# Attention and mixer kernel: the last row tile leaves in two halves of the channels

## The chip, the cores and the metric

The kernel runs on one core of one Trainium2 chip. The metric is the device time of one execution in microseconds (us). The profile of an execution reports its span, which is shorter: in the six runs of the changed kernel the time is 1.75 to 2.5 us longer than the span.

TensorE does the matmuls. VectorE and ScalarE read its sums from PSUM, the memory that holds them. SyncE starts most of the transfers. Rows of a profile name the engines PE, PEld (weight loads), DVE (VectorE), ACT (ScalarE), POOL (GpSimd) and SPq or ACTq (the instruction queues of SyncE and ScalarE).

## The reference

Block-sparse attention over 4 batches, 8 heads, 768 positions and 64 dimensions is followed by a low-rank token mixer and a two-layer perceptron over 512 channels.

```python
scores = scale * np.matmul(q, k.transpose(0, 1, 3, 2))     # scale = 1/8
scores = np.where(mask, scores, -1000000000.0)             # block mask
attn = np.exp(scores - np.max(scores, axis=-1, keepdims=True))
attn = attn / (np.sum(attn, axis=-1, keepdims=True) + 1e-09)
x = heads_side_by_side(np.matmul(attn, v))                 # (4, 768, 512)
h = x.transpose(0, 2, 1) @ U @ V                           # rank 32
u = x + h.transpose(0, 2, 1)
out = u + np.maximum(u @ w_ch1, 0.0) @ w_ch2               # 512 -> 2048 -> 512
```

(`heads_side_by_side` stands for a transpose and a reshape.)

## The kernel before

The kernel interleaves the attention of one batch with the perceptron of the batch before, so that TensorE always has work. Behind the last batch there is no more attention, so its perceptron runs alone at the end. The second layer goes by row tiles of 128 positions, T = 6 to a batch (`...` marks lines left out; comments in the cuts are added). Each gathers 16 matmuls of 512 columns in one PSUM buffer, is added to `xf`, and is stored.

```python
        def w2(sc, part):
            if part == 0:
                hold[sc] = psm([P, HD], FP32)          # sums of a row tile; HD = 512
                ...
            for jj in range(4 * part, 4 * part + 4):
                nc.tensor.matmul(
                    hold[sc],
                    bt.tT[jj][:, sc * P : (sc + 1) * P],
                    w2t[:, jj, :],
                    start=(b > 0 and jj == 0), stop=(jj == NJJ - 1),
                )
            if part == 3:
                of = opool.tile([P, HD], FP32, tag="of", name="of")
                nc.vector.tensor_add(out=of, in0=bt.xf[:, sc, :], in1=hold[sc])
                nc.sync.dma_start(
                    out=out[b].rearrange("(p t) d -> p t d", t=T)[:, sc, :], in_=of
                )
```

`opool` has two buffers and `psm` three. TensorE's order is written by hand; the order on the other engines is the scheduler's.

From the seventh pair of heads on (i = 6, counted from 0), Q and K are turned by transposing transfers from SyncE (`front`): in the traces from `qst` and `kst`, where they lie as loaded, into `qres` and `kres`. In the program they come after the loads of V of a later pair:

```python
            if i + 2 < NPAIR:
                last = load_qk(i + 2)
                load_v(i + 2)
                ...
            if i + 1 < NPE:                            # NPE = 6: turned by TensorE
                ...
            elif i + 1 < NPAIR:
                front(i + 1)                           # turned by transfers
```

The softmax here doesn't subtract the row's maximum and nothing guards it: scores larger than these inputs give would overflow.

Of the kernel before, what the change touches and what calls it, by code (L numbers as in the profile page):

```python
# [9 lines left out]
FP32 = mybir.dt.float32  # L10
# [6 lines left out]
P = 128  # L17
# [3 lines left out]
def kernel(  # L21
# [14 lines left out]
    nc = tc.nc  # L36

    B, H, S, D = q.shape
    BLK = 32
    NB = S // BLK  # L40
    T = S // P
    HD = H * D
# [3 lines left out]
    NJJ = CH // P  # L46
# [45 lines left out]
    opool = ctx.enter_context(tc.tile_pool(name="opool", bufs=2))  # L92
# [11 lines left out]
    def psm(shape, dtype):  # L104
        return psmp.tile(shape, dtype, tag="pm", name="pm")
# [20 lines left out]
    w2t = wpool.tile([P, NJJ, HD], FP16)  # L126
# [20 lines left out]
    def load_v(i):  # L147
# [12 lines left out]
        out=sb[0:NB].rearrange("k z r w -> k (z r w)"),  # L160
        in_=sampled_blocks.bitcast(I32).rearrange("z r -> (z r)")[None, :].broadcast_to(
            [NB, NB * 6]
        ),
# [4 lines left out]
    for h in range(2):  # L168
        for src, nm in ((q, "qld"), (k, "kld")):
            if h == 0:  # L170
# [3 lines left out]
                out=lds[nm][:, h], in_=src[0, h].rearrange("(p t) d -> p t d", t=T)  # L174
# [32 lines left out]
    with tc.manual_schedule(  # L207
# [27 lines left out]
        def first_row(n, c, copy):  # L235
# [14 lines left out]
            out=eq[0:NB], in0=sb[0:NB, :, :, 0], scalar1=iota, scalar2=-1.0,  # L250
# [3 lines left out]
            out=a01[0:NB], in_=eq[0:NB], axis=mybir.AxisListType.X, op=ALU.max  # L254
        )
        nc.vector.scalar_tensor_tensor(
            out=bias[0:NB, :, 0:NB], in0=a01[0:NB, None].broadcast_to([NB, 2, NB]),
# [239 lines left out]
    def mlp_steps(b, bt):  # L497
        def w1(jj, c):
            if c == 0:
                bt.tT.append(tpool.tile([P, S], FP16, tag="tT", name="tT"))  # L500
            pt = psm([P, HS], FP32)
            for cc in range(NCC):
                nc.tensor.matmul(  # L503
                    pt,
                    w1t[:, cc, jj * P : (jj + 1) * P],
                    bt.uT[cc][:, c * HS : (c + 1) * HS],
                    start=(cc == 0), stop=(cc == NCC - 1),
                )
            dst = bt.tT[jj][:, c * HS : (c + 1) * HS]
            if c == 0:  # L510
                nc.scalar.activation(out=dst, in_=pt, func=AF.Relu)  # L511
            else:
                nc.vector.tensor_scalar_max(out=dst, in0=pt, scalar1=0.0)  # L513

        hold = {}

        def w2(sc, part):
            if part == 0:
                hold[sc] = psm([P, HD], FP32)
                if b == 0:  # L520
                    nc.tensor.matmul(  # L521
                        hold[sc], Vt[:, sc, :], bt.a16, start=True, stop=False
# [12 lines that stand above are left out]
                    out=out[b].rearrange("(p t) d -> p t d", t=T)[:, sc, :], in_=of  # L535
                )

        steps = [
            (4 * HS, False, lambda jj=jj, c=c: w1(jj, c))
            for jj in range(NJJ)  # L540
            for c in range(2)
        ]
        steps += [
            (
                (5 if b + part == 0 else 4) * HD,
                part < 3,
                lambda sc=sc, part=part: w2(sc, part),
            )
            for sc in range(T)
            for part in range(4)  # L550
        ]
        return steps


# [36 lines left out]
    with tc.manual_schedule(engines={mybir.EngineType.PE}):  # L591
# [7 lines left out]
        for i in range(NPAIR):  # L599
            b, hp = divmod(i, HP)  # L600
            if hp == 0:
                bt = Batch()
# [59 lines left out]
            if hp == HP - 1:  # L662
                coming = mlp_steps(b, bt)
                mixer.append((slot + 9, lambda coming=coming: queue.extend(coming)))
# [37 lines left out]
```

## Time and profile before

| | before |
|---|---|
| time, median of the first 3 runs | 301.82 us (301.35 to 302.26) |
| span of the profiled run | 298.8 us |
| start of the last addition, to the end of the span | 294.36 us, 4.46 us |

The page of the profile gives the busy time of each engine, its share of the span and its count of instructions.

```profile
PE 291.8 (98%) x2758; PEld 181.2 (61%) x2758; DVE 142.4 (48%) x299; ACT 180.1 (60%) x261; POOL 50.1 (17%) x70
```

TensorE bounds the kernel. The chain of work that ended last, with start, duration and group, shows how it ends.

```profile
252.81 20.80 PE pm L503 x128
273.61 20.73 PE pm L525 x96
294.36 0.69 DVE of L533
```

The 96 matmuls of the last second layer (L525) follow one another without a gap, 20.73 us / 96 = 215.9 ns each, or 3.455 us for a row tile of 16. The last addition starts as they end. The timeline of the last 5 us has start, duration, engine, line, operation, operands and, in brackets, the idle time before and what ended it.

```profile
294.36 0.69 DVE L533 TENSOR_TENSOR of<-xf,pm 128x512 f32<-128x512 f32 x1 [2.76 <-PE pm L525]
295.08 0.33 SPq L534 DMA_DIRECT2D out_dram<-of  x1
```

Narrow windows over the same stretch give the busy time of each engine, then the clock, the busy share of the 16 DMA engines and GB/s.

```profile
295.70:295.90 0.20, 0.00 (x0) 0.00 (x0) 0.00 (x0) 0.00 (x0) 0.00 (x0) 1.00 0.00 0
295.90:296.10 0.20, 0.00 (x0) 0.00 (x0) 0.00 (x0) 0.00 (x0) 0.00 (x0) 1.00 0.92 348
296.10:296.30 0.20, 0.00 (x0) 0.00 (x0) 0.00 (x0) 0.00 (x0) 0.00 (x0) 1.00 0.97 369
296.30:296.50 0.20, 0.00 (x0) 0.00 (x0) 0.00 (x0) 0.00 (x0) 0.00 (x0) 1.00 1.00 379
296.50:296.70 0.20, 0.00 (x0) 0.00 (x0) 0.00 (x0) 0.00 (x0) 0.00 (x0) 1.00 0.59 215
296.70:296.90 0.20, 0.00 (x0) 0.00 (x0) 0.00 (x0) 0.00 (x0) 0.00 (x0) 1.00 0.01 0
```

The bytes of the last store move for only 0.7 us, and start 0.8 us after the issue. This tail is serial: addition, issue, transfer, landing, end of the program. Only work in it, and the matmuls ahead of it, can shorten or lengthen the time here.

### The profile page before, as it was taken

To read this page: it belongs to the slowest core of one execution; us is meant where nothing else is said; L and a number is where in the kernel's file an instruction comes from. 1 tells how busy PE (TensorE), PEld (TensorE's weight loads), DVE (VectorE), ACT (ScalarE), POOL (GpSimd) and SP (SyncE) were. 2 spreads that over 40 slices of the span, in tenths; PEclk is the share of its full clock that TensorE was granted. 3 is DMA by queue.
4 is the path that set the end of the run, shared out by engine and by line. 5 is a ranking of instruction groups with operands and counts; after the bars stand their busy time and mean duration, and the time that the engine had idled before them with its cause. 6 is when DMAs were issued, how large, how long until landed. Compare 5 with 4: busy or idle time off the path is not lost.

```text
span 298.8 us, 6750 instructions
## 1 busy us (share of the span) xinstructions
PE 291.8 (98%) x2758; PEld 181.2 (61%) x2758; DVE 142.4 (48%) x299; ACT 180.1 (60%) x261; POOL 50.1 (17%) x70
## 2 busy tenths in 40 slices
PE   8999999999999999999999999999999999999993
PEld 3677776666665655666665556666665555665441
DVE  7766866347452524454552625345462535443121
ACT  4999997577865665777775565777865530332000
POOL 3783197123223030110202010000000000000000
PEclk9999999999999999999999999999999999999999
DMA  6999989989988485634616271613310122000111
GB/s 185 283 353 238 311 253 235 268 206 218 197 245 178 145 163 147 140 107 64 176 29 141 61 162 53 146 23 46 88 29 35 39 61 72 35 0 2 70 70 71
DMA packets 58519, 39.96 MB, mean 134 GB/s; under 512 B 40136, under 2 KB 54872, under 8 KB 58488
## 3 DMA queue, kind: packets, MB, share of 16 engines
q1 hardware_dynamic: 55764, 35.32, 44.2%
q0 software_dynamic: 2688, 4.19, 7.8%
q8 instruction: 21, 0.34, 0.5%
q14 instruction: 10, 0.08, 0.1%
q10 hardware_dynamic: 36, 0.01, 0.0%
HBM read 27.72 MB, written 6.29 MB: 114 GB/s over the span
## 4 chain that ended last, share of the span: by engine, by line
PE 88%; ACT 9%; issue 1%; DVE 0%; ACTq 0%
PE pm L503 28%; PE pm L525 28%; PE psc L380 17%; ACT est L386 9%; PE pv L420 9%; PE pm L442 2%; PE pm L475 1%; PE psc L218 1%; PE pm L362 0%; PE pm L521 0%; PE pm L491 0%; PE psc L200 0%; DVE of L533 0%; PE pm L452 0%; PE pm L200 0%
## 5 line engine op out<-in xcount | busy, mean ns | idle before, releaser
L386 ACT ACTIVATE est<-psc 128x768 f16<-128x768 f32 x192 | 150.3, 810 | 53.0 <-PE psc L380 52.6
L525 PE MATMUL pm<-w2t,tT 128*128 128x512 f16 x384 | 94.1, 379 | 0.0
L503 PEld LDWEIGHTS <-w1t 128*128 128x128 f16 x512 | 47.1, 98 | 27.0 <-issue 0.3
L420 PEld LDWEIGHTS <-est 128*128 128x128 f16 x1152 | 51.9, 97 | 16.5
L513 DVE TENSOR_SCALAR tT<-pm 128x384 f16<-128x384 f32 x64 | 35.6, 557 | 51.3 <-PE pm L503 48.7
L525 PEld LDWEIGHTS <-tT 128*128 128x128 f16 x384 | 34.8, 98 | 32.0
L511 ACT ACTIVATE tT<-pm 128x384 f16<-128x384 f32 x64 | 31.3, 489 | 37.3 <-PE pm L503 18.7
L380 PE MATMUL psc<-qres_102,kres_104 128*128 128x384 f16 x192 | 46.8, 325 | 1.1 <-ACT est L386 0.9
L380 PE MATMUL psc<-qres_103,kres_105 128*128 128x384 f16 x192 | 46.6, 325 | 0.2
L533 DVE TENSOR_TENSOR of<-xf,pm 128x512 f32<-128x512 f32 x24 | 16.4, 684 | 28.7 <-PE pm L525 28.7
L420 PE MATMUL pv<-vt_99,est 128*128 128x65 f16 x576 | 27.9, 193 | 0.0
L420 PE MATMUL pv<-vt_98,est 128*128 128x65 f16 x576 | 27.8, 193 | 0.0
L380 PEld LDWEIGHTS <-kres_105 128*128 128x128 f16 x192 | 18.3, 98 | 13.6 <-issue 0.5
L380 PEld LDWEIGHTS <-kres_104 128*128 128x128 f16 x192 | 18.0, 97 | 14.0 <-issue 2.0
L429 DVE RECIPROCAL rcp<-pv 128x6 f32<-128x6 f32 x32 | 6.2, 193 | 38.6 <-PE pv L420 38.6
L434 DVE TENSOR_TENSOR xh<-pv,rcp 128x384 f16<-128x384 f32 x32 | 17.8, 557 | 1.0
L434 DVE TENSOR_TENSOR xf<-pv,rcp 128x384 f32<-128x384 f32 x32 | 17.5, 548 | 0.0
L481 DVE TENSOR_TENSOR xf<-xf,pm 128x384 f32<-128x384 f32 x24 | 13.1, 547 | 0.0
L144 POOL CAST qst_101<-qld 128x768 f16<-128x768 f32 x5 | 4.1, 828 | 47.3 <-DMA qres_103<-qst_101 47.3
L144 POOL CAST qst_100<-qld 128x768 f16<-128x768 f32 x5 | 4.1, 827 | 39.9 <-DMA qres_102<-qst_100 39.9
L503 PE MATMUL pm<-uT_207,w1t 128*128 128x384 f16 x32 | 10.4, 326 | 0.0
L503 PE MATMUL pm<-uT_989,w1t 128*128 128x384 f16 x32 | 10.4, 326 | 0.0
(125 smaller groups left out, 298.1 us busy)
## 6 DMA issues: line engine op xcount, KB each, us to landing
vld<-in_v_dram SPq DMA_DIRECT2D x16, 384.0 KB, 7.1
out_dram<-of SPq DMA_DIRECT2D x24, 256.0 KB, 2.0
qld<-in_q_dram SPq DMA_DIRECT2D x15, 384.0 KB, 3.5
kld<-in_k_dram SPq DMA_DIRECT2D x15, 384.0 KB, 6.0
w1t<-in_moe_w_ch_dram POOLq DMA_DIRECT2D x4, 512.0 KB, 9.3
w2t<-in_moe_w_ch_dram POOLq DMA_DIRECT2D x4, 512.0 KB, 12.6
qld<-in_q_dram SPq DMA_DIRECT2D x2, 192.0 KB, 3.3
kld<-in_k_dram SPq DMA_DIRECT2D x2, 192.0 KB, 4.3
```

Source lines behind the costliest of these rows:

```text
L144: last = nc.gpsimd.tensor_copy(out=dst, in_=ld)
L380: nc.tensor.matmul(psc[:, c, 0:HS], kT[:, h, g * P : (g + 1) * P], qT[:, h, c * HS : (c + 1) * HS], start=True, stop=True,)
L386: nc.scalar.activation(out=est.rearrange("k (c n) -> k c n", c=2), in_=psc[:, :, 0:HS], func=AF.Exp, scale=0.125,)
L420: nc.tensor.matmul(pav[:, sc, :], est[:, sc * P : (sc + 1) * P], vts[self.b % 2][:, head, g, 0 : D + 1], start=(g == 0 and sc == 0), stop= ...
L429: nc.vector.reciprocal(out=rcp, in_=pav[:, :, D])
L434: self.last = nc.vector.tensor_tensor(out=dst, in0=pav[:, :, 0:D], in1=rcp[:, :, None].broadcast_to([P, T, D]), op=ALU.mult,)
L481: nc.vector.tensor_add(out=xf, in0=xf, in1=pu)
L503: nc.tensor.matmul(pt, w1t[:, cc, jj * P : (jj + 1) * P], bt.uT[cc][:, c * HS : (c + 1) * HS], start=(cc == 0), stop=(cc == NCC - 1),)
L511: nc.scalar.activation(out=dst, in_=pt, func=AF.Relu)
L513: nc.vector.tensor_scalar_max(out=dst, in0=pt, scalar1=0.0)
L525: nc.tensor.matmul(hold[sc], bt.tT[jj][:, sc * P : (sc + 1) * P], w2t[:, jj, :], start=(b > 0 and jj == 0), stop=(jj == NJJ - 1),)
L533: nc.vector.tensor_add(out=of, in0=bt.xf[:, sc, :], in1=hold[sc])
```

## The change

The intent is to overlap most of the last row tile's addition and store with its own matmuls, and to leave only half an addition and half a store behind the last one. The matmuls of the last row tile split into two groups of 256 columns, each with its own sums, addition and store. The second store goes out on ScalarE's queue.

```diff
+        def last_half(c):
+
+            sc = T - 1
+            po = psm([P, HD // 2], FP32)
+            ch = slice(c * HD // 2, (c + 1) * HD // 2)
+            for jj in range(NJJ):
+                nc.tensor.matmul(
+                    po, bt.tT[jj][:, sc * P : (sc + 1) * P], w2t[:, jj, ch],
+                    start=(jj == 0), stop=(jj == NJJ - 1),
+                )
+            of = opool.tile([P, HD], FP32, tag="of", name="of")
+            nc.vector.tensor_add(out=of[:, ch], in0=bt.xf[:, sc, ch], in1=po)
+            (nc.sync, nc.scalar)[c].dma_start(
+                out=out[b].rearrange("(p t) d -> p t d", t=T)[:, sc, ch], in_=of[:, ch]
+            )
+
...
+        if b == B - 1:
+            steps[-4:] = [(8 * HD, False, lambda c=c: last_half(c)) for c in range(2)]
         return steps
```

## The prediction

> **What bounds the kernel now.** TensorE: the page gives PE 98% busy, and the chain of waits is PE for 88% of the span, at clock 1.00. The chain ends with 96 second-layer matmuls in 20.73 us (215.9 ns each). The change touches only the serial tail behind them: in the timeline the last addition starts at 294.36 us and takes 0.69 us; the store's issue starts at 295.08 and takes 0.33 us. In narrow windows the DMA engines move bytes only from 295.9 to 296.6 (0.70 us, about 370 GB/s). The store lands 2.0 us after its issue, near 297.1; the span ends at 298.8. So 4.4 us lie behind the last matmul, 1.7 us of them after the landing.
>
> **What the change does.** The order of instructions differs only in the last row tile: 16 matmuls of 512 columns become two groups of 16 with 256 columns and the weights loaded twice; one addition becomes two of 256 columns; one store becomes two of 128 KB, the last from ScalarE's idle queue.
>
> **On the critical path.**
> - Matmuls: the columns streamed are the same. Matmuls of 512 and 384 columns start 215.9 and 162.3 ns apart, a line with a fixed term of about 2 ns, so 16 more cost about +0.04 us. The extra weight loads (98 ns busy) should hide: in the timeline 65-column matmuls, each with its own load, start 30 ns apart, far below the 109 ns that I estimate for 256 columns.
> - Last addition: 686 ns for 512 columns, 548 ns for 384 in the groups, so about 415 ns for 256. The Trainium skill, "VectorE: DVE Perf Modes", section on the errata, gives (N+151)/0.96 ns, here 424. Gain 0.27 us.
> - Last store: half the bytes at the same rate, 0.35 us of movement; the fixed part of the 2.0 us stays. Gain 0.25 to 0.35 us.
> - Issue from ScalarE instead of SyncE: its only issue in this trace took 0.60 us, for another shape, against 0.33 us. Cost 0 to 0.27 us.
> - First half: its sums end near 292.6, its store lands near 295.2, before the last store's bytes move. It hides. The second half reuses the buffer whose store lands by 293.6, before its addition at 294.4. The separate queue gains nothing: SyncE is idle by then. The skill's "DMA: Bandwidth & Descriptors", section on issuing engines, agrees: another queue saves only issue time.
>
> **Sum.** −0.27 − 0.30 + 0.04 + 0.13 = −0.40 us, between −0.55 and −0.25: 0.13%, less than the scatter of the three runs (301.35 to 302.26). I predict 301.4 us, 300.8 to 302.0 eight times in ten. Chances: faster by over 2% 0.005, within 2% 0.985, slower by over 2% 0.01.
>
> **What would show it.** Right: the last addition starts at 294.40 ± 0.05 and takes 0.41 to 0.43 us; the last store's bytes move for 0.35 to 0.4 us and land 1.65 to 1.75 us after issue; span 298.3 to 298.6; everything before 291 us unchanged. Wrong: 256-column matmuls over 115 ns apart; a second addition that waits for a store instead of PE; ScalarE's issue over 0.6 us; or an end that lengthens because a second queue must be drained.
>
> **What would make it wrong.** Mostly noise between sessions, larger than the effect; then loads that alternate with matmuls (32 × 98 ns = 3.1 us more), or a slower ScalarE issue, which could cancel the gain.

## The result, and the profile after

| | before | changed |
|---|---|---|
| time, median of 6 fast runs | 301.81 us (300.91 to 302.94) | 301.54 us (300.98 to 302.15) |
| ratio of the fast runs | | 0.9991, 95% interval 0.9967 to 1.0016 |
| span of the profiled run | 298.8 us | 299.1 us |
| start of the last addition | 294.36 us | 295.20 us |
| from there to the end of the span | 4.46 us | 3.87 us |

The fast runs of before are the first three and three more. Ratios are the mean time of one kernel's fast runs over that of the other's of the same rounds, so not quite the ratio of the medians. By the times alone the two kernels are the same; a gain of 0.4 us is smaller than what the interval can resolve. The two traces say more. The end of the chain after the change:

```profile
253.60 20.80 PE pm L503 x128
274.40 17.27 PE pm L525 x80
291.67 3.51 PE pm L544 x32
295.20 0.42 DVE of L549
```

The last row tile (L544) takes 3.51 us instead of 3.455; its matmuls start 109 to 110 ns apart in the trace. But the last first layer (L503) starts at 253.60, not 252.81: 0.79 us were lost before the changed code began. The timeline of the tail:

```profile
293.46 0.42 DVE L549 TENSOR_TENSOR of<-xf,pm 128x256 f32<-128x256 f32 x1 [1.06 <-PE pm L544]
293.90 0.33 SPq L550 DMA_DIRECT2D out_dram<-of  x1
295.20 0.42 DVE L549 TENSOR_TENSOR of<-xf,pm 128x256 f32<-128x256 f32 x1 [1.32 <-PE pm L544]
295.65 0.38 ACTq L550 DMA_DIRECT2D out_dram<-of  x1
```

Both additions wait for PE (the brackets), so neither waits for a store. The first half's addition and issue are over before the second half's sums are. Windows over the last store:

```profile
296.40:296.60 0.20, 0.00 (x0) 0.00 (x0) 0.00 (x0) 0.00 (x0) 0.00 (x0) 1.00 0.22 77
296.60:296.80 0.20, 0.00 (x0) 0.00 (x0) 0.00 (x0) 0.00 (x0) 0.00 (x0) 1.00 0.97 333
296.80:297.00 0.20, 0.00 (x0) 0.00 (x0) 0.00 (x0) 0.00 (x0) 0.00 (x0) 1.00 0.73 241
297.00:297.20 0.20, 0.00 (x0) 0.00 (x0) 0.00 (x0) 0.00 (x0) 0.00 (x0) 1.00 0.02 5
```

The busy shares times 0.2 us add up to 0.39 us of movement, against 0.70 before. So the tail became 0.59 us shorter, as meant, and something earlier took it back in this execution. The waits of TensorE after the first 10 us name it. Columns: engine and line, what it waited for, total us, times, longest. First the kernel before, then the changed one.

```profile
PE psc L380 <- ACT est L386: 0.4, 2, 0.2
```

```profile
PE psc L380 <- DMA kres_104<-kst_106: 0.7, 1, 0.7
PE psc L380 <- ACT est L386: 0.4, 2, 0.2
```

The 0.7 us is one wait near 75 us for the transposed load of K. It lies 216 us ahead of the changed code. TensorE's timeline in the changed kernel:

```profile
75.93 0.50 PE L380 MATMUL psc<-qres_102,kres_104 128*128 128x384 f16 x2 [0.68 <-DMA kres_104<-kst_106]
```

More can be read from the two traces. Every engine has the same instructions in the same order in both, up to the last row tile. So each matmul of one can be set against the same matmul of the other: the changed kernel runs 0.05 us early at 74 us, 0.80 us late at 78 us, and 0.80 us late still at 270 us. The whole loss arose at that one wait.

### The profile page after: what moved, and what is told of

Read it like the earlier page. It is cut to its first block, busy times and chain, and to the rows that moved or that the text cites. A ratio compares the mean times of both kernels' runs of the same rounds, so it can differ in the third digit from the quotient of the medians.

```text
span 299.1 us, 6786 instructions
## 1 busy us (share of the span) xinstructions
PE 292.0 (98%) x2774; PEld 182.8 (61%) x2774; DVE 142.5 (48%) x300; ACT 180.2 (60%) x261; POOL 50.1 (17%) x70
## 4 chain that ended last, share of the span: by engine, by line
PE 87%; ACT 9%; DMA 1%; issue 1%; DVE 0%; ACTq 0%
PE pm L503 27%; PE pm L525 27%; PE psc L380 17%; ACT est L386 9%; PE pv L420 9%; PE pm L442 2%; DMA kres_104<-kst_106 1%; PE pm L475 1%; PE psc L218 1%; PE pm L544 1%; PE pm L362 0%; PE pm L521 0%; PE psc L200 0%; PE pm L491 0%; PE pm L452 0%
## 5 line engine op out<-in xcount | busy, mean ns | idle before, releaser
L525 PE MATMUL pm<-w2t,tT 128*128 128x512 f16 x368 | 90.7, 379 | 0.0
L503 PEld LDWEIGHTS <-w1t 128*128 128x128 f16 x512 | 47.1, 98 | 27.0 <-issue 0.3
L525 PEld LDWEIGHTS <-tT 128*128 128x128 f16 x368 | 33.3, 98 | 30.1
L533 DVE TENSOR_TENSOR of<-xf,pm 128x512 f32<-128x512 f32 x23 | 15.7, 684 | 25.9 <-PE pm L525 25.9
L503 PE MATMUL pm<-uT_207,w1t 128*128 128x384 f16 x32 | 10.4, 325 | 0.0
L503 PE MATMUL pm<-uT_3050,w1t 128*128 128x384 f16 x32 | 10.4, 326 | 0.0
```

What stands on the lines that cost most here:

```text
L503: nc.tensor.matmul(pt, w1t[:, cc, jj * P : (jj + 1) * P], bt.uT[cc][:, c * HS : (c + 1) * HS], start=(cc == 0), stop=(cc == NCC - 1),)
L525: nc.tensor.matmul(hold[sc], bt.tT[jj][:, sc * P : (sc + 1) * P], w2t[:, jj, :], start=(b > 0 and jj == 0), stop=(jj == NJJ - 1),)
```

## The experiments

Theory T: the tail is shorter by what its parts say, about 0.5 us net, and a wait near 75 us that comes and goes hides it. Its rivals: R, the change itself causes that wait or lengthens something else; Q, the queue of its own is what helps. Twelve runs were made in three calls; the times of two of them are of a single execution, whose state is unknown. All gave correct results. Kernels are compared only within the same rounds. A run over 1.5% above the fastest of the same kernel is called slow; times below are medians of the other, fast runs. "The tail" is the time from the start of the last addition to the end of the span.

### The changed kernel and the kernel before, again

No edit.

> The changed kernel once more, beside the kernel before on one chip. Theory T (the tail gets about 0.5 us shorter, and a wait for the transposed K load near 75 us, which comes and goes from run to run, hides it): from the start of the last addition to the end of the span 3.8 to 4.0 us against 4.4, ratio 0.998 to 0.999. Rival R (the change also lengthens something before 291 us): the start of the last addition is again 0.5 us or more later than the 294.36 us of before, in this profile too, and with the same wait.

Measured: 301.73 us against 301.97, ratio 0.9989 (0.9959 to 1.002). The tail is 3.88 us again. TensorE waited 1.63 us near 75 us, and the last addition started at 296.05, as rival R expects too. So this run confirms the tail and does not separate T from R.

> The kernel before against itself. Every profile of a changed kernel so far showed TensorE waiting 0.7 to 2.2 us near 75 us for the transposed K load, the first profile of before none. Theory T (the wait comes and goes and has nothing to do with the change): this profile of before has a wait there as well, above 0.3 us, the span less that wait is 298.6 to 299.0 us, and the ratio to itself is off 1 by up to 0.3%. Rival R (the change causes the wait): no wait again, and a start of the last addition at 294.2 to 294.6 us.

Measured: 302.52 us against 302.46 for the same kernel (one slow run left out on each side), ratio 0.9979 (0.9936 to 1.0022). The profile fell in the slow state (span 303.8 us) and had a wait of 3.05 us there; its span less that wait is 300.8 us and misses the expectation. Being slow, it decides nothing.

> The kernel before once more, one look, since its last profile fell in the slow state. Theory T (the wait near 75 us belongs to the kernel before as well): a wait of TensorE for the transposed K load of 0.3 us or more, and span less wait 298.5 to 299.0 us, if the state is fast. Rival R (the change causes it): no wait.

Measured: one run of 301.88 us (span 300.1, state unknown), and the waits of TensorE are these.

```profile
PE psc L380 <- DMA kres<-kst: 0.7, 1, 0.7
PE psc L380 <- ACT est L386: 0.6, 3, 0.2
```

The unchanged kernel has the wait too, and rival R falls in its main form: the wait is not the change's. Its other form, that the change lengthens something else ahead of the tail, falls by the matmuls set against each other as above. In all seven profiles of a change on this order of loads, TensorE's lead or lag against the first profile of before moves by over 0.05 us in two places only: in the first 12 us (to between -0.16 and +0.30 us) and at that wait. Span less wait is 299.4 us, above the 299.0 expected; this execution also was 0.4 us later than the first profile at 8 us already (its third pair of score matmuls started at 8.67 us, against 8.26). The interval of the kernel against itself, about 0.4% (1.3 us) to each side, shows that timing alone could not have found 0.5 us here.

### Both half stores from SyncE

```diff
-            (nc.sync, nc.scalar)[c].dma_start(
+            nc.sync.dma_start(
```

> Both half stores issued by SyncE. Theory T says that the queue of its own is worth nothing: the last issue takes 0.33 us instead of 0.38, the tail from the last addition is 3.8 to 3.9 us, the ratio like that of the changed kernel within 0.1%. Rival Q (the second queue is what lets the last store leave early): the last store starts to move bytes 0.2 us or more later after the end of its addition than with ScalarE's queue.

Measured: 301.12 us against 301.97, ratio 0.9971 (0.9945 to 0.9997), with a wait of 1.07 us near 75 us. The tail is 3.77 us, 0.1 us shorter than with ScalarE's queue: the issue took 0.33 instead of 0.38 us, so landing came 1.71 instead of 1.76 us after its start, and the end followed 1.61 instead of 1.66 us after that. The bytes of the last store start 0.85 us after the end of its addition, against 0.91 with ScalarE's queue, so not later. Rival Q falls; the queue of its own gains nothing. Two details missed: the tail was expected at 3.8 to 3.9 us, and the ratio within 0.1% of the changed kernel's (0.9989), which the intervals cannot resolve.

### One store, sums and additions by halves

```diff
+            of = whole[0]                              # one buffer for both halves
             nc.vector.tensor_add(out=of[:, ch], in0=bt.xf[:, sc, ch], in1=po)
-            (nc.sync, nc.scalar)[c].dma_start(... ch ...)
+            if c == 1:
+                nc.sync.dma_start(... all of the row tile, in_=of)
```

> Sums and additions by halves, one store of all 256 KB after the second addition. Isolates the addition. Theory T: last addition 0.42 us instead of 0.69, bytes move 0.70 us as before, tail from its start 4.15 to 4.25 us (before 4.44, changed 3.87). If the halving of the store is worth nothing, the tail is 3.9 us.

Measured: 302.33 us against 301.97, ratio 1.002 (0.9979 to 1.006), with a wait of 2.21 us near 75 us in the profile. Its tail:

```profile
296.69 0.42 DVE L553 TENSOR_TENSOR of<-xf,pm 128x256 f32<-128x256 f32 x1 [1.33 <-PE pm L546]
297.14 0.33 SPq L555 DMA_DIRECT2D out_dram<-of  x1
```

The tail is 4.18 us: 0.28 us shorter than before (4.46), which is the addition (0.42 instead of 0.69 us). The store landed 2.02 us after the start of its issue, exactly as before. The halved addition is thus worth 0.27 us. The rest, 0.30 us, comes with the halved store, ScalarE's issue and one check fewer at the end (below) included.

### One group of sums, addition and store by halves

```diff
+                n = 2 if b == B - 1 and sc == T - 1 else 1
+                for c in range(n):                     # addition and store of each half
```

> One group of sums of 512 columns, addition and store by halves. Isolates the separate sums. Theory T: both additions wait for all sums and follow one another, 0.42 us each; from the start of the first addition to the end of the span 4.25 to 4.35 us, against 4.44 before and 3.87 with the sums apart, so most of the gain goes. Rival (only the smaller last store counts, not when the sums end): 4.0 us or less.

Measured: one run of 300.66 us (state unknown), without a wait near 75 us. The timeline of its tail:

```profile
294.66 0.75 DVE L536 TENSOR_TENSOR of<-xf,pm 128x256 f32<-128x256 f32 x2 [2.76 <-PE pm L525]
295.11 0.33 SPq L539 DMA_DIRECT2D out_dram<-of  x1
295.45 0.39 ACTq L539 DMA_DIRECT2D out_dram<-of  x1
```

The two additions stand in a row behind all the sums, 0.75 us together. From the start of the first to the end of the span it is 4.22 us, just under the range expected and 0.24 us less than before; with the sums apart it is 3.87. So 0.35 of the 0.59 us come from the first half leaving early, and they need sums of their own. (One profile of each; the tails of like kernels agree to 0.03 us here.)

### Channels cut 384 and 128

```diff
-            po = psm([P, HD // 2], FP32)
-            ch = slice(c * HD // 2, (c + 1) * HD // 2)
+            ch = (slice(0, 384), slice(384, HD))[c]
+            po = psm([P, ch.stop - ch.start], FP32)
```

> The changed kernel with channels cut 384 and 128 instead of 256 and 256. Theory T, with the terms of the changed kernel's profile: last addition 0.29 us, last 64 KB move in about 0.2 us, tail from its start 3.55 to 3.65 us; the 32 matmuls take 3.5 us as with halves. If the weight loads no longer hide behind 128 columns, the 16 last matmuls start over 65 ns apart. If short rows cost the store, its bytes move for 0.3 us or more.

Measured: 300.97 us against 301.97, ratio 0.9968 (0.9938 to 0.9998), with a wait of 1.96 us near 75 us. Its tail:

```profile
296.37 0.29 DVE L549 TENSOR_TENSOR of<-xf,pm 128x128 f32<-128x128 f32 x1 [0.34 <-PE pm L544]
296.69 0.38 ACTq L550 DMA_DIRECT2D out_dram<-of  x1
```

The last addition took 0.29 us and the tail 3.56 us, 0.31 us less than with halves. The row tile took 3.51 us on TensorE as with halves, so weight loads hide behind 128 columns too: the 16 last matmuls start 56 ns apart. The short rows cost the store nothing: its packets kept the 16 DMA engines busy for 0.22 us. This cut is near its limit: VectorE stood idle for only 0.34 us between the two additions, and the last store's bytes began 0.01 us after the first part's had ended. A still smaller last part would, by these figures, soon wait for one of them; it was not run.

### All six row tiles of the last batch by halves

```diff
-            steps[-4:] = [(8 * HD, False, lambda c=c: last_half(c)) for c in range(2)]
+            steps[-4 * T :] = [
+                (8 * HD, False, lambda c=c, sc=sc: last_half(c, sc))
+                for sc in range(T)
+                for c in range(2)
+            ]
```

> All six row tiles of the last batch by halves: what the split costs, six times over. Theory T: each row tile takes 3.51 us instead of 3.455 on TensorE, so the six take 21.06 us against 20.73, that is 0.3 us more; tail 3.87 us as in the changed kernel. If an addition or a store holds up the next group's sums (rival), TensorE idles between the groups and the six take 21.3 us or more.

Measured: 301.30 us (three fast runs; a fourth, of 304.85, was slow) against 302.46, ratio 0.9947 (0.9882 to 1.0012), with a wait of 1.65 us near 75 us. The chain shows the six row tiles in 20.97 us, against 20.73:

```profile
275.37 20.97 PE pm L543 x192
296.37 0.42 DVE of L548
```

The split costs 0.04 us a row tile, and the rival falls. The tail was the surprise: 3.15 us instead of 3.87. Landing came 1.72 us after the start of the issue, against 1.76. What shrank is the time from landing to the end, from 1.66 to 0.98 us. SyncE's semaphore instructions in the trace say how (a semaphore is a counter by which one engine or transfer tells another that it is done). At the end SyncE checks a list of completion semaphores in turn, 0.07 us each and one gap of about 0.39 us. In most kernels the store that lands last is near the head of that list, and the rest is checked after it has landed; here it was near the end of the list. The table is worked out from the records of SyncE's instructions (us); "landed" is when SyncE's check of that store passed, and that check is counted.

```
kernel     issue of last store   landed   checks from its   list done   end of span
                                          own on
before     295.08                297.10   8                 297.99      298.83
changed    295.65                297.41   7                 298.23      299.07
all six    296.82                298.54   2                 298.68      299.52
```

From the end of the list to the end of the span it is 0.83 to 0.84 us in all 14 profiles. With 8 checks left, landing to the end of the list takes 0.87 to 0.90 us (6 profiles), with 7 left 0.79 to 0.84 (7 profiles), with 2 left 0.14. So the end follows the list, and how much of it is left when the last store lands sets the time. No run changed only that place.

### A quiet base: the transposed loads ahead of the loads of V

SyncE's timeline shows its transfers issued one behind the other. Before, the stretch ahead of the transposed loads is this (`vld` is a buffer for V as loaded):

```profile
48.43 20.30 SPq L150 DMA_DIRECT2D vld<-in_v_dram  x5
68.90 1.72 SPq L350 DMA_TRANSPOSE qres_102<-qst_100  x1
71.18 1.44 SPq L350 DMA_TRANSPOSE kres_104<-kst_106  x1
```

Five loads of V, each waiting for a free buffer, hold the queue for 20 us. A buffer is free when GpSimd has cast what it holds, and the trace shows these casts wait for the load itself: one issued at 48.43 was cast from 62.92 on. So the transposed K needed near 75 us is issued only at 71. The edit puts the loads of V from i = 7 on behind the transposed loads of the pair before. It has nothing to do with the change studied here.

```diff
-                load_v(i + 2)
+                if i + 1 >= NPE:
+                    tr = front(i + 1)                  # front now returns its last transfer
+                    with tc.issue_after(tr.ins):
+                        load_v(i + 2)
+                else:
+                    load_v(i + 2)
...
-            elif i + 1 < NPAIR:
+            elif i + 2 == NPAIR:
                 front(i + 1)
```

> The kernel before, without the change, with the loads of V from pair 7 on placed after the transposed loads of the next pair, so that these are not held up behind them in SyncE's queue. Theory T (the wait near 75 us is what scatters the time): no wait of TensorE for the transposed load, span 298.5 to 299.0 us, time 0.3 to 0.5% under before, and less scatter. If later V loads come too late, a wait for vt in the second product appears instead and the time grows.

Measured: 300.43 us against 302.46, ratio 0.9934 (0.99 to 0.9969), somewhat more than expected; the tail is 4.45 us as before. Five of the six runs lie between 300.26 and 300.58, one at 302.22. SyncE's timeline, and the waits of TensorE:

```profile
58.49 2.09 SPq L350 DMA_TRANSPOSE qres<-qst  x1
60.75 3.18 SPq L350 DMA_TRANSPOSE kres<-kst  x1
63.98 0.57 SPq L150 DMA_DIRECT2D vld<-in_v_dram  x1
```

```profile
PE psc L381 <- ACT est L387: 0.4, 2, 0.2
```

K is issued 10 us earlier, the wait is gone, and five of six runs agree to 0.3 us, where the ten fast runs of the kernel before scattered from 301.13 to 304.89 us in these rounds. On this base the change can be seen. Both of the next kernels ran in the same rounds.

> The quiet base without the change, again, to stand beside the next kernel in the same rounds. Theory T: median 300.3 to 300.7 us, no wait near 75 us, tail from the last addition 4.4 us.

> The quiet base with exactly the change (halves, stores from SyncE and ScalarE). If the change is worth what the tail says, 0.56 us less 0.06 us of TensorE, this kernel is 0.4 to 0.6 us faster than the quiet base in the same rounds, that is 0.13 to 0.2%; span 297.9 to 298.1 us. If something else of the change costs time, the two agree within 0.2 us.

Measured, all runs in us: without the change 302.21, 300.62, 300.65, 300.82, 302.22, 300.33 (median 300.74); with it 299.98, 300.85, 300.53, 300.20, 299.83, 300.45 (median 300.33). All twelve runs are fast. The first median is 0.04 us above the range expected, and the span of the profiled run with the change, 298.2 us, 0.1 above. The kernel before had 302.12 in these rounds; the ratios to it are 0.9975 (0.995 to 1.0) and 0.995 (0.993 to 0.997). The medians differ by 0.41 us. The two runs at 302.2 us are another thing: the profile fell on one of them, and its first matmuls were slow. TensorE's timeline near 6 us, without the change and then with it:

```profile
5.82 0.49 PE L225 MATMUL pv<-small,bias 24*128 24x384 f16 x1
6.24 0.53 PE L200 MATMUL pm<-id,stkld 128*64 128x128 f16 x3
6.70 0.50 PE L225 MATMUL pm<-small,bias 24*128 24x384 f16 x1
```

```profile
5.58 0.33 PE L225 MATMUL pv<-small,bias 24*128 24x384 f16 x1
5.84 0.35 PE L200 MATMUL pm<-id,stkld 128*64 128x128 f16 x3
6.13 0.33 PE L225 MATMUL pm<-small,bias 24*128 24x384 f16 x1
```

The same matmuls take about 1.5 times as long at the start of that execution. Against the first profile of the quiet base, TensorE is 1.94 us late from 10 us on, and no more than that to the end. The other run at 302.2 us has the same span of 300.4 us but no profile, so its cause is assumed. Leaving those two runs out, which was decided after seeing them, the spans are 298.6 to 299.1 us without the change and 298.0 to 298.6 with it; their means, 298.8 (four runs) and 298.2 (six), differ by 0.6 us. Both figures agree with the 0.54 us of the traces (0.59 us of tail less 0.055 us of matmuls), within what so few runs can tell. The fast profiles agree as well; these are the last addition of the first quiet base (span 298.49 us), and the tail with the change (span 298.21 us):

```profile
294.03 0.69 DVE L534 TENSOR_TENSOR of<-xf,pm 128x512 f32<-128x512 f32 x1 [2.76 <-PE pm L526]
```

```profile
294.31 0.42 DVE L550 TENSOR_TENSOR of<-xf,pm 128x256 f32<-128x256 f32 x1 [1.33 <-PE pm L545]
294.76 0.38 ACTq L551 DMA_DIRECT2D out_dram<-of  x1
```

The tails are 4.45 and 3.89 us, 0.56 apart. TensorE was 0.24 us later with the change from 45 us on already, and 0.04 us more are the last row tile; together they give the 0.28 us by which the spans differ.

### All together

The quiet base with channels cut 384 and 128, and both stores from SyncE.

> The change with channels cut 384 and 128, both stores from SyncE, and the V loads after the transposed loads. Theory T adds the terms: tail from the last addition 3.45 to 3.5 us, TensorE's last row tile plus 0.05 us, no wait near 75 us; span 297.7 to 298.1 us, time 0.6 to 0.7% under before.

Measured: 299.98 us against 302.46, ratio 0.9914 (0.9882 to 0.9946), all six runs between 299.47 and 300.95. The span is 297.7 us and the tail 3.52 us, 0.02 above the range expected. It is faster than both kernels, most of it by the order of the loads and not by the tail.

## Why the prediction was right or wrong

The time, 301.54 us, lay in the range (300.8 to 302.0) and near the 301.4 predicted, and "the same within 2%" was right. That the time came so near is luck: the wait near 75 us, which the prediction does not have, moves it by 0 to over 2 us from run to run, and the interval holds no gain as well as 0.4 us. What the experiments bear out is the mechanism of the tail. Point by point:

- Matmuls: +0.055 us for the last row tile, 0.04 for each of six, against +0.04. The loads hide: the matmuls of 256 columns start 109 to 110 ns apart. The Trainium skill, "TensorE: Matmul & The Clock Gate", section "Back-to-back issue gap", gives N/2.4 + 2.5 ns for an isolated matmul, here 109.2; the trace agrees, with a weight load for each. The same section's lower figures for sustained streams (about 131 ns at 512 columns) do not fit these 215.9 ns.
- Last addition: 0.42 us against 0.41 to 0.43, and 0.29 us for 128 columns. The skill's rule in "VectorE: DVE Perf Modes", section on the TRN2 errata, (N+151)/0.96 ns, gives 0.424 and 0.291 us; the trace agrees.
- Last store: the bytes moved for 0.39 us, against 0.35 to 0.4. Landing from SyncE came 1.71 us after the start of the issue, against 2.02 for the whole: 0.31 us gained, the term said 0.30.
- Issue from ScalarE: 0.05 us more, against 0 to 0.27 us with 0.13 entered. This term was too large; with the end of the program (next point) it is why the sum said 0.40 us and the traces show 0.54. The prediction took it from a transfer of another shape. The skill's "DMA: Bandwidth & Descriptors", section "Issuing engines are not separate DMA queues", says that another queue saves only the issue time; here SyncE was idle, so there was none to save, and both stores from SyncE were 0.1 us better.
- The end of the program after landing was held constant. It shrank by 0.07 us, as one check fewer was left, and in the run with six split row tiles by 0.75 us against before.
- "Everything before 291 us unchanged", the start of the last addition at 294.40 and a span of 298.3 to 298.6 failed: 295.20 and 299.1. The one profile of before happened to have no wait near 75 us, and it was read as if every execution ran so. Of the other profiles with that order of loads, all but one (the run with one group of sums) have it: 0.66 us in the second look at the unchanged kernel (3.05 in the slow first one), 0.68 to 2.21 in those with the change or a part of it. The prediction named noise between sessions as the chief risk but put it down to sessions, where it comes and goes from run to run within one.

What stays open: why some executions start with slow matmuls, why the loads ahead of the transposed K land sooner or later from run to run, and what sets the place of the last store in SyncE's list.

## What to carry to other kernels

When the end of a program is a serial chain of sums, addition, store and landing, cut the last piece unevenly so that little is left behind the last matmul, and give the early piece sums of its own; here it cost only a few hundredths of a microsecond, as the weight loads hid, and shortened the tail by 0.59 us cut in halves and by 0.90 cut 384 and 128. A gain of that size can't be seen in times that scatter by 2 us: compare the stage in several traces, or first remove the wait that scatters. Look for that wait in more than one profile, since one execution may not show it, and look at what stands ahead of the late transfer in its queue.

## What the Trainium skill lacked or had wrong

- "Runtime: NRT & Kernel Launch", the preamble and postamble breakdown, gives the barrier that the runtime adds behind a kernel about 1.5 us as one item. No page tells of the checks with which the program itself ends. Here the landing of the last store to the end of the span took 1.73 us, of which 0.89 us were SyncE's checks of completion semaphores one by one, and 0.98 us in all where the last store was near the end of that list. That the order of the checks matters stands nowhere.
- "DMA: Bandwidth & Descriptors", anatomy of one DMA, fits a fixed cost of about 2.0 us for transfers from GpSimd. For stores from SyncE, 2.02 us for 256 KB and 1.71 us for 128 KB leave about 1.4 us fixed, issue included (a line through the two; for 64 KB it gives 1.56 us, and the last run measured 1.57). The page has no such fit for this path (only a latency to the first byte), and does not give the issue from ScalarE or SyncE (0.38 and 0.33 us).
- "TensorE: Matmul & The Clock Gate", part 1, lets the clock fall after an idle window of about 3.4 us, while its closing table warns of gaps over about 3 us. In the slow profile of the unchanged kernel a wait of 3.05 us was enough, which fits the table and not the window: the clock granted to TensorE, as a share of full speed, was 0.68 from 78.4 to 80 us and 0.50 from 80 to 82 us, right after it; a wait of 2.21 us in another kernel left it at 1.00. That is one slow run, and explains no difference above.
- The same page, section "Back-to-back issue gap", gives sustained streams with weight loads about 81 ns at 128 columns and 131 ns at 512. Here 16 matmuls of 128 columns start 56 ns apart and 96 of 512 columns 215.9 ns, each with its own weight load.
- The same page names the clock's rise at the start as varying from run to run, and warns that clock records can be unreliable. The records of the slow start show a granted clock of 1.00 from 4.7 to 8 us, while matmuls took 0.49 instead of 0.33 us: either the records are off there, or something other than the clock slowed them. No run tells which.
